# Hash attention followed by a squared-ReLU layer: where the first pair prepares the second pair

## The chip, the cores and the metric

The kernel runs on one core of a Trainium2 chip. The metric is the device time of one execution in microseconds (us). TensorE (PE in the profile) multiplies matrices, VectorE (DVE) and ScalarE (ACT) work element by element, GpSimd (POOL) does a little set-up, and SyncE (SP) issues most of the DMAs. Each engine works through its own instructions in the order in which they were issued[...].

## What is computed

The reference, cut to what matters (4 batches, 8 heads, 768 positions, head width 64, 6 hash bits; 3072 tokens, model width 512, hidden width 2048):

```python
q_bits = (np.einsum('bhsd,dk->bhsk', q, proj) > 0)
k_bits = (np.einsum('bhsd,dk->bhsk', k, proj) > 0)
q_bucket = np.sum(q_bits * powers, axis=-1)        # the same for k_bucket
mask = q_bucket[:, :, :, None] == k_bucket[:, :, None, :]
scores = scale * np.matmul(q, k.transpose(0, 1, 3, 2))
scores = np.where(mask, scores, -1000000000.0)
attn = softmax(scores)
attn_out = np.matmul(attn, v)
x = attn_out.transpose(0, 2, 1, 3).reshape(B * S, H * D)
h = x @ w_in
out = np.maximum(h, 0.0) ** 2 @ w_out
```

A query sees only the keys that have the same six sign bits as itself.

## The kernel before

The kernel has two stages. The first, some 335 us long, is the attention; the second multiplies its result by the two weight matrices. The change touches only the very beginning of the first stage.

**Pairs and blocks.** Two heads are treated together as a pair; there are NP = 16 pairs, and the loop at L606 runs over them. In a pair the 768 keys fall into six blocks of 128. `score(pr, kt)` (L386) makes the scores of one key block against all 768 queries: into a PSUM tile of 512 columns and one of 256 (per head), each from a product of the bit rows (`bits`, bf16) and a product of the features (`feat`, the transposed q and k). ScalarE then takes the exponential of each of the two tiles (L413) into a buffer `e`. `attend(pr, kt)` (L432) multiplies a block of `e` with the values `v_nat`. `add_up(pr, kt)` (L419) adds the blocks up on VectorE for the softmax's denominators; its first call, with kt = 1, adds blocks 0 and 1 (L423), and later calls add one more block (L428).

**What the next pair needs.** `features(pr, w)` (L330) transposes the loaded q (w = 0) or k (w = 1) of a pair on VectorE, into tiles with two buffers. `hash_bits(pr, banks)` (L337) multiplies both with the projection, four products for q and four for k, into one PSUM tile named `hash`. `signs` (L351) turns the result into bit rows with eight ScalarE activations. `weigh` (L379) scales the key bits, in place, with one more. Inside the loop, `prepare()` (L610) is `hash_bits` and `signs` for the pair that follows. For pair 0 itself this work is done ahead of the loop, with `first_features` and `first_keys`.

**PSUM.** The tiles named `st`, `hash`, `tot` and `tp` are all taken in turn from one set of three (`turn`, L104). A new one therefore waits until the third one before it has been read, as a rule by ScalarE.

**The order.** The order is written out by hand (`tc.manual_schedule()`, L584): every engine gets its instructions as the Python calls come. In pair 0 it is: scores of block 0, the second half of the first key bits, scores of block 1, `add_up(0, 1)`, `features(1, 0)` and `features(1, 1)`, `part_weight(0)` (two VectorE steps of a weight conversion, L143 and L147), scores of blocks 2 and 3, `prepare()`, `place_power(0)` (its two ScalarE steps, L160 and L161), `attend` for blocks 0 and 1, `add_up` for blocks 2 and 3, `round_weight(0)` (three VectorE steps, L171, L176, L179), `part_weight(1)`, scores of blocks 4 and 5, `weigh(1)`, `place_power(1)`, `attend` for blocks 2 and 3, `add_up` for blocks 4 and 5. Pair 1 begins with `features(2, w)`, `round_weight(1)` and the scores of its blocks 0 and 1; then `finish(0)` does `prepare()` for pair 2, the sums of the denominators (`tot`, L457) and the last two `attend` of pair 0.

**Data.** The q and k of pair 1 are loaded by `load_pair(1)` (L287): eight DMAs on SP's queue, ahead of the loop.

Of the kernel before, what the change touches and what calls it, by code (L numbers as in the profile page):

```python
# [34 lines left out]
def kernel(  # L35
# [68 lines left out]
    def turn(name):  # L104

        return ps_s.tile([P, 2, 512], FP32, name=name, tag="turn")
# [16 lines left out]
    def load_weight(i):  # L123
        src, r, c = pieces[i]
        if src.dtype != U64:
            goals[i] = goal(i)
            nc.sync.dma_start(out=goals[i], in_=src[r:r + P, c:c + PIECE])
            return
        raw = p_w.tile([P, PIECE, 2], U32, name="raw", bufs=3)
        nc.sync.dma_start(  # L130
            out=raw.rearrange("p f w -> p (f w)"),
            in_=src.bitcast(U32)[r:r + P, 2 * c:2 * (c + PIECE)],
        )
        raws[i] = raw
# [28 lines left out]
    def round_weight(i):  # L163

        raw = raws.pop(i, None)
        if raw is None:
            return keep_weight(i)
        goals[i] = goal(i)
        low, high = raw[:, :, 0], raw[:, :, 1]
        power, top = parts.pop(i)  # L170
        nc.vector.scalar_tensor_tensor(  # L171
            out=power, in0=high, scalar=0x80000000, in1=power,
            op0=ALU.bitwise_and, op1=ALU.bitwise_or,
        )
        one = top.bitcast(FP32)
        nc.vector.scalar_tensor_tensor(  # L176
            out=one, in0=low, scalar=2.0**-32, in1=top, op0=ALU.mult, op1=ALU.add,
        )
        nc.vector.scalar_tensor_tensor(  # L179
            out=goals[i], in0=one, scalar=2.0**-20, in1=power.bitcast(FP32),  # L180
            op0=ALU.mult, op1=ALU.mult,
        )
        keep_weight(i)
# [95 lines left out]
    def load_pair(pr):  # L279


        b, j = divmod(pr, PB)
        for src, name in ((q, "q_nat"), (k, "k_nat")):
            t = p_qk.tile([P, S], FP32, name=name)
            for g in range(4):
                h, e = divmod(g, 2)
                nc.sync.dma_start(  # L287
                    out=t[g * 32:(g + 1) * 32].rearrange("i (c d) -> i c d", d=32),
                    in_=src[b, 2 * j + h].rearrange("(c i) (e d) -> e i c d", i=32, e=2)[e],
                )  # L290
            nat[pr, name] = t
# [38 lines left out]
    def features(pr, w):  # L330

        feat[pr, w] = p_f.tile([P, S], FP32, name=f"feat{w}")
        nc.vector.transpose(out=feat[pr, w], in_=nat[pr, ("q_nat", "k_nat")[w]])
# [3 lines left out]
    def hash_bits(pr, banks, ws=(0, 1), cs=(0, 1)):  # L337


        for w in ws:  # L340
            hashed[pr, w] = banks
            for c in cs:
                g = 2 * w + c
                for h in range(2):
                    rows = slice(h * D, (h + 1) * D)
                    nc.tensor.matmul(  # L346
                        out=banks[g * NR_B:(g + 1) * NR_B, h, 0:HS], lhsT=projs[rows],
                        rhs=feat[pr, w][rows, c * HS:(c + 1) * HS], start=True, stop=True,
                    )

    def signs(pr, w):  # L351
        bits[pr, w] = t = all_bits[pr % 2][w]
        for c in range(2):
            at = slice((2 * w + c) * NR_B, (2 * w + c + 1) * NR_B)
            for h in range(2):
                nc.scalar.activation(  # L356
                    out=t[h * D:h * D + NR_B, c * HS:(c + 1) * HS], in_=hashed[pr, w][at, h, 0:HS],
                    func=ACTF.Sign, scale=HUGE, bias=lifts[at],
                )
# [19 lines left out]
    def weigh(pr):  # L379

        t = bits[pr, 1]
        nc.scalar.activation(out=t, in_=t, func=ACTF.Copy, scale=gains)
# [3 lines left out]
    def score(pr, kt):  # L386

        e = ring[len(weights) % NRING]
        weights[pr, kt] = e
        key = slice(kt * P, (kt + 1) * P)  # L390
        sts = []

        def products(st, lo, hi, src, first):
            for h in range(2):
                rows = slice(h * D, (h + 1) * D)
                nc.tensor.matmul(  # L396
                    out=st[:, h, 0:hi - lo], lhsT=src[pr, 1][rows, key],
                    rhs=src[pr, 0][rows, lo:hi], start=first, stop=not first,
                )


        if (pr, kt) == (0, 0):
            for lo, hi in CUTS:
                sts.append(turn("st"))
                products(sts[-1], lo, hi, feat, True)
        for i, (lo, hi) in enumerate(CUTS):
            if len(sts) <= i:
                sts.append(turn("st"))
                products(sts[i], lo, hi, bits, True)
                products(sts[i], lo, hi, feat, False)  # L410
            else:
                products(sts[i], lo, hi, bits, False)
            nc.scalar.activation(  # L413
                out=e[:, :, lo:hi], in_=sts[i][:, :, 0:hi - lo], func=ACTF.Exp, scale=scale
            )
# [107 lines left out]
    def sums_in(c):  # L523

        j, h = divmod(c, 2)
        t, at = ins[j], slice(h * NS, (h + 1) * NS)
        nf = NFT // 2
        sums = [p_t.tile([P, nf, NS], FP32, name=f"s_in{n}", bufs=2) for n in range(4)]
        sums_a(
            t[:, 0:nf, 0, at], t[:, nf:NFT, 0, at], t[:, 0:nf, 1, at], t[:, nf:NFT, 1, at], *sums  # L530
        )
        for n in range(4):
            put_factor(3 + n, c * NS, sums[n])
# [9 lines left out]
    def load_x(i):  # L543

        x = p_c.tile([P, NFT, NCH], FP32, name="x")
        nc.gpsimd.dma_start(out=x, in_=x_all[:, :, i * NCH:(i + 1) * NCH])
        xs[i] = x, [p_c.tile([P, 2, NCH // 2], FP32, name=f"t_x{n}") for n in range(3)]
# [23 lines left out]
    def finish(pr, beside=None):  # L571

        tot = turn("tot")
        if beside:
            beside()
        sum_up(pr, tot)
        if pr == NP - 1:
            sum_x(0, 2)
            sum_x(0, 3)
        for kt in (SB - 2, SB - 1):  # L580
            attend(pr, kt)
        spread(pr)

    with tc.manual_schedule():  # L584
# [21 lines left out]
        for pr in range(NP):  # L606
            a, b = 2 * pr, 2 * pr + 1
            more = pr + 1 < NP

            def prepare():  # L610

                hash_bits(pr + 1, turn("hash"))
                for w in (1, 0):
                    signs(pr + 1, w)


            if pr + 2 < NP:
                load_pair(pr + 2)
            if pr == X_0:
                load_x(0)  # L620
            if not more:
                sums_in(3)
            if more and pr > 0:
                for w in range(2):
                    features(pr + 1, w)
            if pr > 0:
                round_weight(b - 2)
                load_weight(b)
            score(pr, 0)
            if pr == 0:  # L630
                first_keys(1, turn("hash"))
            score(pr, 1)
            if pr > 0:
                finish(pr - 1, prepare if more else None)
            add_up(pr, 1)
            if pr == 0:
                for w in range(2):
                    features(1, w)
            if pr > 0:
                normalize(pr - 1)  # L640


            if pr == X_0 + 1:
                for n in range(2):
                    load_unit(n)
            part_weight(a)
            score(pr, 2)
            score(pr, 3)
            if pr == 0:
                prepare()  # L650
            elif more:
                weigh(pr + 1)
            place_power(a)
            attend(pr, 0)
            attend(pr, 1)
            for kt in (2, 3):
                add_up(pr, kt)
            if more:
                load_values(pr + 1)


            round_weight(a)
            part_weight(b)
            if more:
                load_weight(a + 2)
            score(pr, 4)
            score(pr, 5)
            if pr == 0:
                weigh(1)
            place_power(b)  # L670
            attend(pr, 2)
            attend(pr, 3)
            add_up(pr, 4)

            if pr not in sums:
                add_up(pr, 5)
            if pr in sums:
                sums_in(sums[pr])
# [801 lines left out]
```

## Time and profile before

| | |
|---|---|
| time, median of 4 runs | 884.41 us (883.28 to 885.53) |
| the profiled execution | 883.89 us, of which the span of the profile is 882.1 us |
| granted TensorE clock, mean | 0.997 |
| 12 to 17 us: busy PE, DVE, ACT | 4.91, 3.48, 3.94 of 5.00 us |
| 17 to 22 us | 4.40, 4.90, 3.62 |
| 22 to 27 us | 3.42, 2.01, 4.88 |
| 27 to 32 us | 5.00, 4.90, 4.21 |
| 32 to 37 us | 5.00, 4.79, 4.75 |

Pair 0 fills about the first 30 us of the span and pair 1 the next 20. The five windows show how the load stands on the engines around the place of the change; the granted clock is 1.00 in all five. In the timelines that are shown in the prediction, a row gives the start of a run of like instructions (us from the start of the span), the time from the start of the first to the end of the last, the engine, the line, the operation, the tiles written and read, the number, and in brackets for how long the engine was idle before and who, by the profile, released it.

### The profile page before, as it was taken

The numbers are of one execution on the slowest core, as the hardware profiler recorded it, in microseconds if no ns is written. First come the engines' busy times: TensorE is split into PE (matmuls) and PEld (weight loads), VectorE is DVE, ScalarE is ACT, GpSimd is POOL, SyncE is SP. The second block draws the span as 40 slices with busy tenths as digits, with TensorE's granted clock in tenths as the row PEclk, the third lists the DMA queues.
The fourth block names the chain that finished last, engine by engine and source line by source line (L and its number), as shares of the span: only waits on it lengthen the run. The fifth ranks groups of instructions, "written<-read, shape, count | busy, mean of one in ns | idle before, by whom it ended". The sixth has DMA issues, their size and how long they took to land.

```text
span 882.1 us, 12164 instructions
## 1 busy us (share of the span) xinstructions
PE 867.6 (98%) x4364; PEld 520.2 (59%) x4364; DVE 755.9 (86%) x1096; ACT 391.7 (44%) x673; POOL 107.0 (12%) x172
## 2 busy tenths in 40 slices
PE   8999999999999999999999999999999999999996
PEld 4444444444444444444688875556888755568885
DVE  5899999999999998888779978888889788888875
ACT  5988888888888861222211123332111233321110
POOL 2000000000000000564222021111100211110002
PEclk9999999999999999999999999999999999999998
DMA  9678779899778545989897775436857744455565
GB/s 183 128 151 134 195 183 189 181 280 208 153 166 187 160 143 194 305 258 289 283 350 246 183 162 171 160 116 228 291 144 186 172 157 156 129 166 153 158 176 102
DMA packets 224131, 167.09 MB, mean 189 GB/s; under 512 B 164448, under 2 KB 181344, under 8 KB 224064
## 3 DMA queue, kind: packets, MB, share of 16 engines
q1 hardware_dynamic: 189152, 87.19, 41.2%
q0 software_dynamic: 12528, 41.30, 15.1%
q10 hardware_dynamic: 22384, 37.76, 14.3%
q8 instruction: 36, 0.59, 0.3%
q14 instruction: 31, 0.25, 0.1%
HBM read 124.52 MB, written 41.68 MB: 188 GB/s over the span
## 4 chain that ended last, share of the span: by engine, by line
PE 95%; DVE 2%; ACT 1%; issue 1%; DMA 0%; DVEq 0%
PE acc L708 40%; PE st L396 17%; PE acc L927 16%; PE xo L438 13%; PE acc L880 5%; PE tot L457 2%; PE hash L346 1%; DVE total L428 1%; ACT e L413 1%; ACT bits L356 1%; PE xo L326 0%; PE tp L309 0%; DMA w_in<-s_in 0%; DVE out_piece L179 0%; DVE power L171 0%
## 5 line engine op out<-in xcount | busy, mean ns | idle before, releaser
L413 ACT ACTIVATE e<-st 128x1024 f32<-128x1024 f32 x192 | 145.2, 810 | 46.9 <-PE st L396 42.7
L396 PE MATMUL st<-feat,feat 64*128 64x512 f32 (+1 forms) x768 | 150.4, 483 | 0.0
L438 PE MATMUL xo<-e,v_nat 128*64 128x512 f32 (+1 forms) x768 | 134.8, 492 | 0.0
L708 PE MATMUL acc<-b,leaf 128*128 128x256 f32 x600 | 133.4, 379 | 1.1 <-issue 1.1
L708 PEld LDWEIGHTS acc<-b,leaf 128*128 128x128 f32 x600 | 113.7, 190 | 17.9 <-issue 2.7
L428 DVE TENSOR_TENSOR total<-total,e 128x1536 f32<-128x1536 f32 x61 | 107.2, 1757 | 4.4
L438 PEld LDWEIGHTS xo<-e,v_nat 128*64 128x64 f32 x768 | 51.3, 136 | 82.4 <-issue 75.3
L927 PE MATMUL acc<-t_x,w_unit 128*128 128x512 f32 x192 | 90.2, 592 | 0.0
L396 PEld LDWEIGHTS st<-feat,feat 64*128 64x128 f32 x768 | 66.0, 188 | 33.7 <-issue 24.1
L708 PE MATMUL acc<-t,leaf 128*128 128x256 f32 x336 | 76.2, 380 | 0.0
L356 ACT ACTIVATE bits<-hash,lifts 32x384 bf16<-32x384 f32 x120 | 68.6, 572 | 3.2 <-issue 1.3
L708 PEld LDWEIGHTS acc<-t,leaf 128*128 128x128 f32 x336 | 63.7, 190 | 9.1 <-DVE t L519 0.5
L792 DVE SCALAR_TENSOR_TENSOR b<-h 128x512 f32<-128x512 f32 x96 | 65.7, 691 | 3.0
L396 PE MATMUL st<-bits,bits 64*128 64x256 bf16 (+1 forms) x384 | 63.1, 325 | 1.8 <-ACT e L413 1.4
L927 PE MATMUL acc<-x,w_unit 128*128 128x512 f32 x128 | 60.2, 592 | 0.0
L708 PE MATMUL acc<-x,w_unit 128*128 128x512 f32 x128 | 56.6, 594 | 0.0
L708 PE MATMUL acc<-b_t,leaf 128*128 128x256 f32 x240 | 53.8, 379 | 0.0
L927 PEld LDWEIGHTS acc<-t_x,w_unit 128*128 128x128 f32 x192 | 36.5, 190 | 28.9 <-issue 26.8
L715 ACT COPY two<-acc 128x256 f32<-128x256 f32 (+1 forms) x29 | 12.5, 431 | 87.7 <-PE acc L708 63.0
L715 ACT COPY one<-acc 128x256 f32<-128x256 f32 (+1 forms) x29 | 12.5, 431 | 86.2 <-PE acc L708 57.7
L708 PEld LDWEIGHTS acc<-b_t,leaf 128*128 128x128 f32 x240 | 45.5, 190 | 6.2
L396 PEld LDWEIGHTS <-bits 64*128 64x128 bf16 x384 | 23.4, 93 | 41.6 <-issue 37.9
(161 smaller groups left out, 1170.4 us busy)
## 6 DMA issues: line engine op xcount, KB each, us to landing
leaf<-w_out ACTq DMA_DIRECT2D x142, 256.0 KB, 3.1
w_unit<-w_in SPq DMA_DIRECT2D x16, 640.0 KB, 4.0
raw<-in_moe_w_in_dram SPq DMA_DIRECT2D x16, 512.0 KB, 5.5
raw<-in_moe_w_out_dram SPq DMA_DIRECT2D x16, 512.0 KB, 4.4
w_unit<-w_in SPq DMA_DIRECT2D x8, 896.0 KB, 8.1
w_out<-sums POOLq DMA_DIRECT2D x16, 448.0 KB, 6.8
sum<-w_in SPq DMA_DIRECT2D x16, 448.0 KB, 4.8
v_nat<-in_v_dram SPq DMA_DIRECT2D x16, 384.0 KB, 4.4
```

What stands on the lines that cost most here:

```text
L346: nc.tensor.matmul(out=banks[g * NR_B:(g + 1) * NR_B, h, 0:HS], lhsT=projs[rows], rhs=feat[pr, w][rows, c * HS:(c + 1) * HS], start=True, ...
L356: nc.scalar.activation(out=t[h * D:h * D + NR_B, c * HS:(c + 1) * HS], in_=hashed[pr, w][at, h, 0:HS], func=ACTF.Sign, scale=HUGE, bias=li ...
L396: nc.tensor.matmul(out=st[:, h, 0:hi - lo], lhsT=src[pr, 1][rows, key], rhs=src[pr, 0][rows, lo:hi], start=first, stop=not first,)
L413: nc.scalar.activation(out=e[:, :, lo:hi], in_=sts[i][:, :, 0:hi - lo], func=ACTF.Exp, scale=scale)
L428: nc.vector.tensor_tensor(out=totals[pr], in0=totals[pr], in1=weights[pr, kt][:, :, 0:S], op=ALU.add)
L438: nc.tensor.matmul(out=xo[h * D:(h + 1) * D, lo:hi], lhsT=nat[pr, "v_nat"][:, h, kt * D:(kt + 1) * D], rhs=weights[pr, kt][:, h, lo:hi], s ...
L457: nc.tensor.matmul(out=tot[g * 32:(g + 1) * 32, 0:HS], lhsT=ones, rhs=src[:, h, c * HS:(c + 1) * HS], start=src is srcs[0], stop=src is sr ...
L708: nc.tensor.matmul(out=acc[to], lhsT=a(i), rhs=b(i), start=first and i == 0, stop=last and i == n - 1, skip_group_check=True,)
L715: nc.scalar.copy(out=t, in_=acc[of])
L792: nc.vector.scalar_tensor_tensor(out=out, in0=h, scalar=0.0, in1=h, op0=ALU.max, op1=ALU.mult)
L880: nc.tensor.matmul(out=out, lhsT=w[:, a], rhs=b, start=start, stop=stop, skip_group_check=True)
L927: nc.tensor.matmul(out=acc[to], lhsT=w[:, PLACE[a], f], rhs=bt[b](f), start=first and f == 0, stop=last and f == NFT // 2 - 1, skip_group_ ...
```

## The change

Two steps of pair 0 are moved; nothing is added or taken out. The two `features(1, w)` now stand ahead of `add_up(0, 1)` on VectorE. The `prepare()` for pair 1, which followed the scores of the fourth block (kt = 3), now stands ahead of them. For the other pairs the order is the same: the second hunk only rewrites the condition for `weigh`.

```diff
@@ -630,12 +630,12 @@
             if pr == 0:
                 first_keys(1, turn("hash"))
             score(pr, 1)
+            if pr == 0:
+                for w in range(2):
+                    features(1, w)
             if pr > 0:
                 finish(pr - 1, prepare if more else None)
             add_up(pr, 1)
-            if pr == 0:
-                for w in range(2):
-                    features(1, w)
             if pr > 0:
                 normalize(pr - 1)
 
@@ -645,10 +645,10 @@
                     load_unit(n)
             part_weight(a)
             score(pr, 2)
-            score(pr, 3)
             if pr == 0:
                 prepare()
-            elif more:
+            score(pr, 3)
+            if more and pr > 0:
                 weigh(pr + 1)
             place_power(a)
             attend(pr, 0)
```

In the two programs' instruction lists this gives: on TensorE the 8 hash products move ahead of the 8 score products (and their weight loads) of the fourth block; on ScalarE the 8 sign activations move ahead of the fourth block's two exponentials; on VectorE the two transposes move ahead of the first sum. GpSimd's and SP's lists are the same in both.

## The prediction

> **What bounds the kernel.** I read the page's busy shares and its chain first, then the timelines of TensorE, ScalarE and VectorE over the first 60 us.
>
> ```profile
> span 882.1 us, 12164 instructions
> PE 867.6 (98%) x4364; PEld 520.2 (59%) x4364; DVE 755.9 (86%) x1096; ACT 391.7 (44%) x673; POOL 107.0 (12%) x172
> PE 95%; DVE 2%; ACT 1%; issue 1%; DMA 0%; DVEq 0%
> ```
>
> TensorE is busy for 98% of the span, and the chain that ended last is 95% TensorE. So only TensorE's idle time, 14.5 us in all, can be won. Pair 0 holds part of it:
>
> ```profile
> 16.40 0.29 PE L396 MATMUL st<-bits,bits 64*128 64x256 bf16 x2
> 16.51 0.61 PE L396 MATMUL st<-feat,feat 64*128 64x256 f32 x4
> 17.72 1.62 PE L346 MATMUL hash<-feat,projs 64*32 64x384 f32 x16 [0.60 <-ACT e L413]
> 19.27 2.81 PE L438 MATMUL xo<-e,v_nat 128*64 128x512 f32 x16
> 22.01 0.39 PE L396 MATMUL st<-bits,bits 64*128 64x512 bf16 x2
> ...
> 24.17 0.39 PE L396 MATMUL st<-bits,bits 64*128 64x512 bf16 x2 [0.37 <-ACT bits L356]
> ...
> 26.63 0.29 PE L396 MATMUL st<-bits,bits 64*128 64x256 bf16 x2 [1.21 <-ACT e L413]
> ...
> 33.36 1.11 PE L346 MATMUL hash<-feat,projs 64*32 64x384 f32 x16
> 34.40 0.85 PE L457 MATMUL tot<-total,ones 128*32 128x384 f32 x8
> ```
>
> There are three waits: 0.60 us before the hash products (and a stretched 1.62 us for them), 0.37 before the sixth block's first tile, 1.21 before its second. The two other engines tell why:
>
> ```profile
> 13.38 4.75 ACT L413 ACTIVATE e<-st 128x1024 f32<-128x1024 f32 x6 [0.85 <-PE st L396]
> 19.45 4.66 ACT L356 ACTIVATE bits<-hash,lifts 32x384 bf16<-32x384 f32 x8 [1.32 <-issue]
> 24.14 0.72 ACT L160 ACTIVATE small<-power,excess 128x512 uint8<-128x512 uint32 x1
> 24.90 0.63 ACT L161 ACTIVATE power<-small 128x512 uint32<-128x512 uint8 x1
> 25.55 2.92 ACT L413 ACTIVATE e<-st 128x1024 f32<-128x1024 f32 x4
> ```
>
> ```profile
> 14.93 1.76 DVE L423 SCALAR_TENSOR_TENSOR total<-e,e 128x1536 f32<-128x1536 f32 x1 [1.47 <-ACT e L413]
> 16.60 0.97 DVE L333 STREAM_TRANSPOSE feat<-q_nat 128x768 f32<-128x768 f32 x1
> 17.50 0.94 DVE L333 STREAM_TRANSPOSE feat<-k_nat 128x768 f32<-128x768 f32 x1
> ```
>
> VectorE stood idle for 1.47 us, did the first sum, and only then the transposes, which end at 17.57 and 18.43. TensorE, through with the fourth block, could have begun the hash at about 16.95 (a block takes 15.33 to 13.71, 1.62 us, and this one began at 15.33). It began the q half at 17.72 and the k half only at 18.49, 0.05 after the k transpose. The profile names an exponential as the releaser of the first wait, but that tile's buffer was last read by the third block's second exponential, which ended at 16.51; it was the q transpose. The signs followed 0.96 after the k half began: ScalarE, which has work without a pause from 19.45, lost 1.32 us. The 1.21 us wait at 26.63 hangs on it: the sixth block's second tile needs the PSUM tile whose exponential started at 25.55, behind signs and power.
>
> **The change, part by part.** All durations come from this execution.
>
> *Transposes first (VectorE).* VectorE is free at 13.45. The last k DMA of pair 1 was issued at 8.33 and took 3.99 us to land, 12.3; the q ones are earlier. So the transposes run 13.46 to 15.29 (1.83 us, as before from 16.60 to 18.43). The first sum needs the second block's exponentials, done at 14.89; it goes from 14.92 to 15.22. Only VectorE waits for it. Then come part_weight(0) (0.72), whose data landed at 15.2, and the third block's sum, 17.5 to 19.3.
>
> *Hash between third and fourth block (TensorE).* The third block ends at 15.33; k is ready at 15.29 plus 0.05. The hash starts at 15.34 and takes 0.80 (pair 2 shows it unhindered: 53.50 to 54.30). Its buffer, the second block's, is free at 14.89. The fourth block goes from 16.14 to 17.76; its tiles come free at 16.02 and 16.51. The products with the values (2.74, from 19.27 to 22.01) end at 20.50.
>
> *Signs before the fourth block's exponentials (ScalarE).* They are ready at 15.34 + 0.96 = 16.30, while the third block's exponentials run until 16.51: no gap. Signs 16.53 to 21.19, the fourth block's exponentials to 22.8. From 13.38 to the fifth block's exponential ScalarE has the same work as before and no pause. So this exponential starts 1.32 earlier, at 24.23.
>
> *The price.* On TensorE the fifth block's first tile now takes the buffer of the hash, so it waits for the last sign: from 20.50 to about 21.25, a new wait of 0.75. It is covered, as the sixth block's second tile still waits for the fifth block's exponential: 26.63 less 1.32 = 25.31. Everything on TensorE from there stands 1.32 earlier; pair 1 begins at 28.70 instead of 30.02, its hash at 32.04 instead of 33.36. On VectorE the fourth block's sum stood ready at 20.85 and now waits for 22.8; behind it are queued round_weight(0), part_weight(1), two sums and the transposes of pair 2. It ends at 24.58. Then round_weight(0), whose power is there at 25.53 - 1.32 = 24.21, starts at 24.55 instead of 25.56. **VectorE wins only 1.0.**
>
> *What is late next.* Pair 1's hash waited for VectorE before: its k half could not start until the transpose was through at 33.56, and 34.40 - 33.36 is 1.04 against 0.80 unhindered, 0.24 lost. Now k is ready at 33.56 - 1.0 = 32.56 while TensorE arrives at 32.04. The loss grows to 32.56 + 0.05 - 32.04 = 0.57, so `tot` follows at 33.40 instead of 34.40. Sum: 1.32 - (0.57 - 0.24) = **1.0 us**. After it nothing holds the gain: in pair 2 VectorE waits 0.65 for TensorE, ScalarE up to 1.7, and all pairs and the second stage follow TensorE. SP's list is unchanged; the earlier transposes only free buffers that its loads reach at 22.3 anyway.
>
> **A rule that speaks against it.** The Trainium skill, "ScalarE: Activation LUTs", section "What ACT_TABLE_LOAD costs", says that each switch to another function set costs about 2.66 us (1283 ns and a drain). The change puts signs between exponentials: one more trip away from Exp and back, two switches. By the rule that is up to 5.3 us, and the sum becomes a loss of about 4. But the rows by line show ACT_TABLE_LOAD once in the whole span (1283 ns at 2.59 us), and between exponentials and signs of pair 1 only 0.08 us. The functions lie in one set here; I take zero.
>
> **Forecast and rivals.** Profiled execution 883.89, less 1.0: 882.9. The median stands 0.52 above it: 884.41 - 1.0 = **883.4 us**. What a measurement can tell from no change is 0.2%, 1.8 us.
>
> *A, as worked out, 0.55:* gain 0.9 to 1.35 (the upper end if VectorE doesn't hold pair 1's hash), 883.0 to 883.5.
>
> *B, more is won, 0.25:* besides the hash wait (18.49 - 16.95 = 1.54) the 0.37 goes too, 1.9 in all: 882.5, faster beyond 0.2%. All waits of pair 0 and pair 1's 0.24 give 3.4 at most, 881.0. For it: the signs are done almost 3 us earlier. Against: ScalarE's work up to the fifth block's exponential leaves no room for more than 1.32.
>
> *C, the hash is late, slower, 0.08:* TensorE works in order, so if k of pair 1 isn't there, the fourth block's scores, its exponentials and its sum all queue behind the hash, where before they passed ahead. Every us by which k is late after 15.3 costs one: the sum is nothing at a lateness of 1.0 (landing at about 15.4), and 0.2% slower at 2.8 (about 17.2), 886.2. For it: a k DMA took 3.5 to 5.6 us to land. Against: even 5.6 from 8.33 gives 13.9, before the 14.36 at which its transpose would begin.
>
> *D, nothing moves the end, 0.12:* VectorE in pair 1 takes the whole gain: if its fourth sum ends at 25.5 rather than 24.58, the hash of pair 1 is no earlier than before. 884.4.
>
> **The numbers.** Faster takes most of B and a little of A through scatter, 0.26; slower is C and a rest of D, 0.08; within 0.2% 0.66. The range, 882.0 to 884.9, holds A, D and B's 882.5, with the 1.1 us by which single runs of before lie off their median; it leaves out C and B's far end.
>
> **What would show it.** After: the transposes begin at 13.5 and the first sum near 15.2; hash products at 15.3 in about 0.8; no ScalarE pause ahead of the signs at 16.5; a new wait of 0.75 on TensorE at 20.5, one of about 1.3 ending at 25.3; pair 1's first scores at 28.7, its hash taking 1.3 to 1.4, `tot` at 33.4. Wrong if `tot` stands within 0.3 of 34.40 (D), or ahead of 32.9 (B), or if the transposes begin after 14 (C).

## The result and the profile after

The changed kernel takes 882.54 us, the median of 40 runs (881.82 to 883.62), against 883.88 us for the kernel before (60 runs, 883.12 to 885.53). The ratio is 0.9985, with a 95% interval of 0.9981 to 0.9990: between 0.9 and 1.7 us are won, a gain that is there but smaller than the 0.2% that was named as the bound.

The head of the page of the kernel after:

```profile
span 880.7 us, 12164 instructions
PE 866.6 (98%) x4364; PEld 519.7 (59%) x4364; DVE 755.7 (86%) x1096; ACT 391.7 (44%) x673; POOL 107.1 (12%) x172
```

The busy times are those of before to 1.0 us. From the second block's first scores to pair 2's `tot`, TensorE was busy for 40.03 of 42.21 us before and for 39.58 of 41.07 us after. So 0.69 us of idle time went; the other 0.45 had counted as busy, mostly because hash products that wait for their operand inside the group are counted so. In this execution pair 0 ran 0.34 us later than in the profile of before: the second block's first scores start at 12.43 and not at 12.09, behind a later load of pair 0's k. All times below are to be read against that. Three rows of TensorE's timeline of before that the prediction does not show (second block, pair 1's first scores, pair 2's `tot`):

```profile
12.09 0.39 PE L396 MATMUL st<-bits,bits 64*128 64x512 bf16 x2 [0.24 <-ACT e L413]
...
30.02 0.39 PE L396 MATMUL st<-bits,bits 64*128 64x512 bf16 x2
...
54.30 0.85 PE L457 MATMUL tot<-total,ones 128*32 128x384 f32 x8
```

TensorE's timeline of the kernel after, from there to pair 2's `tot`:

```profile
12.43 0.39 PE L396 MATMUL st<-bits,bits 64*128 64x512 bf16 x2 [0.22 <-ACT e L413]
...
15.78 0.88 PE L346 MATMUL hash<-feat,projs 64*32 64x384 f32 x16
...
21.60 0.39 PE L396 MATMUL st<-bits,bits 64*128 64x512 bf16 x2 [0.49 <-ACT bits L356]
...
25.46 0.29 PE L396 MATMUL st<-bits,bits 64*128 64x256 bf16 x2 [0.99 <-ACT e L413]
...
28.86 0.39 PE L396 MATMUL st<-bits,bits 64*128 64x512 bf16 x2
...
32.19 1.47 PE L346 MATMUL hash<-feat,projs 64*32 64x384 f32 x16
33.59 0.85 PE L457 MATMUL tot<-total,ones 128*32 128x384 f32 x8
...
53.50 0.85 PE L457 MATMUL tot<-total,ones 128*32 128x384 f32 x8
```

The hash runs without a wait in 0.88 us (before: a wait of 0.60 and then 1.62). The wait of 0.37 for the last sign, which stood before the sixth block, is replaced by one of 0.49 before the fifth, and pair 1's hash is stretched from 1.11 to 1.47 us. ScalarE's timeline shows where the gain is made:

```profile
13.72 3.13 ACT L413 ACTIVATE e<-st 128x1024 f32<-128x1024 f32 x4 [0.85 <-PE st L396]
16.88 4.67 ACT L356 ACTIVATE bits<-hash,lifts 32x384 bf16<-32x384 f32 x8
21.57 1.51 ACT L413 ACTIVATE e<-st 128x1024 f32<-128x1024 f32 x2
...
23.87 0.63 ACT L161 ACTIVATE power<-small 128x512 uint32<-128x512 uint8 x1
24.41 2.90 ACT L413 ACTIVATE e<-st 128x1024 f32<-128x1024 f32 x4
```

No bracket stands behind the signs any more: the 1.32 us of idling ahead of them are gone. VectorE's timeline shows the price, first before (the third and the fourth block's sums in one row, and pair 2's k transpose), then after:

```profile
19.00 3.61 DVE L428 TENSOR_TENSOR total<-total,e 128x1536 f32<-128x1536 f32 x2
...
32.63 0.93 DVE L333 STREAM_TRANSPOSE feat<-k_nat 128x768 f32<-128x768 f32 x1
```

```profile
13.72 0.97 DVE L333 STREAM_TRANSPOSE feat<-q_nat 128x768 f32<-128x768 f32 x1
14.62 0.94 DVE L333 STREAM_TRANSPOSE feat<-k_nat 128x768 f32<-128x768 f32 x1
...
23.12 1.76 DVE L428 TENSOR_TENSOR total<-total,e 128x1536 f32<-128x1536 f32 x1 [3.59 <-ACT e L413]
24.80 0.69 DVE L171 SCALAR_TENSOR_TENSOR power<-raw,power 128x512 uint32<-128x512 uint32 x1
...
31.83 0.94 DVE L333 STREAM_TRANSPOSE feat<-k_nat 128x768 f32<-128x768 f32 x1
```

The fourth block's sum waits 3.59 us for exponentials that stand behind the signs, and all that is queued behind it, down to the k transpose of pair 2 at 31.83, is late for TensorE, whose hash begins at 32.19 and gets its k at 32.77 only.

### The profile page after: what moved, and what is told of

It is laid out like the page before. It is cut to its first block, busy times and chain, and to the rows that moved or that the text cites. A ratio compares the mean times of both kernels' runs of the same rounds, so it can differ in the third digit from the quotient of the medians.

```text
span 880.7 us, 12164 instructions
## 1 busy us (share of the span) xinstructions
PE 866.6 (98%) x4364; PEld 519.7 (59%) x4364; DVE 755.7 (86%) x1096; ACT 391.7 (44%) x673; POOL 107.1 (12%) x172
## 4 chain that ended last, share of the span: by engine, by line
PE 94%; DVE 2%; ACT 1%; DMA 1%; issue 0%; ACTq 0%; DVEq 0%
PE acc L708 40%; PE st L396 17%; PE acc L927 16%; PE xo L438 13%; PE acc L880 5%; PE tot L457 2%; PE hash L346 2%; DVE total L428 1%; DMA k_nat<-in_k_dram 1%; ACT e L413 1%; ACT bits L356 1%; DMA w_in<-s_in 0%; DVE out_piece L179 0%; DVE power L171 0%; ACT small L160 0%
```

## The experiments

The differences are of the size of a run's scatter, so two readings are kept beside each other: the median (11 runs of each experiment, 40 of the full change) against the kernel before on the same chip, and, in one profiled execution, two stretches of TensorE's timeline. Both begin with the second block's first scores (12.09 in before); one ends with pair 1's first scores (30.02), the other with pair 2's `tot` (54.30). They leave out the start and the second stage, which differ from one execution to the next by some tenths of a us and more. Two programs were profiled in two executions each (the full change and e8); each gave its stretches again to 0.01 us.

| kernel | median, us | of before | ratio (95%) | to pair 1 | to pair 2's tot |
|---|---|---|---|---|---|
| before | 883.88 | | | 17.92 | 42.21 |
| full change | 882.54 | 883.88 | 0.9985 (0.9981 to 0.9990) | 16.42 | 41.07 |
| e1 transposes only | 882.35 | 883.83 | 0.9981 (0.9972 to 0.9990) | 16.64 | 40.91 |
| e2 hash only | 885.42 | 883.83 | 1.0017 (1.0008 to 1.0026) | 19.98 | 44.62 |
| e3 full, pair 2 early | 882.21 | 883.83 | 0.9979 (0.9970 to 0.9988) | 16.41 | 40.83 |
| e4 transposes, pair 2 early | 882.66 | 883.83 | 0.9984 (0.9975 to 0.9993) | 16.62 | 41.04 |
| e5 full, late loads | 884.77 | 883.79 | 1.0010 (1.0001 to 1.0019) | 18.38 | 43.03 |
| e6 before, late loads | 883.44 | 883.79 | 0.9996 (0.9987 to 1.0005) | 17.93 | 42.18 |
| e7 transposes, part early | 882.23 | 883.79 | 0.9981 (0.9972 to 0.9990) | 16.62 | 40.68 |
| e8 full, part between | 881.72 | 883.79 | 0.9978 (0.9969 to 0.9987) | 16.42 | 40.47 |
| e9 full change again | 882.59 | 883.65 | 0.9991 (0.9982 to 1.0000) | 16.42 | 41.07 |
| e10 as e8, again | 881.67 | 883.65 | 0.9977 (0.9968 to 0.9986) | 16.42 | 40.47 |

**Which half of the change does it?** First each half alone. e1 moves the transposes only:

```diff
             score(pr, 1)
+            if pr == 0:
+                for w in range(2):
+                    features(1, w)
...
             add_up(pr, 1)
-            if pr == 0:
-                for w in range(2):
-                    features(1, w)
```

> Only the two transposes of pair 1 are moved ahead of the first sum; the hash products stay behind the fourth block's scores. My theory (what is won is ScalarE's pause of 1.32 us ahead of the signs): the transposes end at about 15.3, so the hash runs at once behind the fourth block, near 17.0, and its result is there about when the fourth block's exponentials end at 18.1. The pause is gone as in the full change, and the fourth block's sum on VectorE doesn't wait for the signs, so pair 1's hash loses 0.24 us as before and not 0.56: 1.3 us faster than before, 0.15 to 0.3 us faster than the full change; on TensorE no wait of 0.5 before the fifth block's first tile. Rival (the place of the hash between the third and fourth block brings the gain): about as before, at most 0.5 us faster.

TensorE's timeline of e1, and the signs in ScalarE's:

```profile
17.14 0.88 PE L346 MATMUL hash<-feat,projs 64*32 64x384 f32 x16
...
22.97 0.39 PE L396 MATMUL st<-bits,bits 64*128 64x512 bf16 x2 [0.49 <-ACT bits L356]
...
32.16 1.09 PE L346 MATMUL hash<-feat,projs 64*32 64x384 f32 x16
```

```profile
18.24 4.67 ACT L356 ACTIVATE bits<-hash,lifts 32x384 bf16<-32x384 f32 x8
```

ScalarE's pause ahead of the signs is gone here too. The stretch to pair 2's `tot` is 1.30 us shorter than before, 0.16 shorter than with the full change, and pair 1's hash takes 1.09, about the 1.11 of before. The rival falls: the hash's new place is not what brings the gain. As expected, there is no wait before the fifth block's first tile; the wait for the last sign (0.49) stands at the sixth block's first tile (22.97), where before had 0.37. The e2 kernel moves the other half:

```diff
             score(pr, 2)
-            score(pr, 3)
             if pr == 0:
                 prepare()
-            elif more:
+            score(pr, 3)
+            if more and pr > 0:
                 weigh(pr + 1)
```

> Only the hash products and signs are moved between the third and the fourth block's scores; the transposes stay behind the first sum and end at 18.43. My theory: the hash can't start its k half before 18.49, the fourth block's scores queue behind it on TensorE and its exponentials behind the signs (24.1), so the fifth block's exponential starts at about 27.0 in place of 25.55: 1.5 to 2.0 us slower than before. Rival (the hash's new place brings the gain): faster by 0.5 us or more.

```profile
17.69 2.28 PE L346 MATMUL hash<-feat,projs 64*32 64x384 f32 x16 [2.21 <-DVE feat L333]
```

```profile
20.08 4.66 ACT L356 ACTIVATE bits<-hash,lifts 32x384 bf16<-32x384 f32 x8 [3.59 <-issue]
```

In these rows of TensorE's and ScalarE's timelines of e2 the hash waits 2.21 us for the q transpose. Its k half begins at 18.46, 0.05 after the k transpose, but the signs follow only 1.62 later, where before they followed after 0.96. Beside the missing 0.66 stands a lower clock: in windows of 1 us the granted clock is 1.00 up to 18 us, 0.75 from 18 to 19, 0.50 from 19 to 21, 0.54 from 21 to 22, and 1.00 again after. In no other trace of the twelve is it under 1.00 in the first 56 us. With the fourth block's scores queued behind the hash, pair 1 starts some 2.05 late, and pair 2's `tot` follows 2.42 late. Less the 0.66, an estimate, that would be about 1.8, within the expected 1.5 to 2.0; the median shows 1.6 (0.7 to 2.3). In how many of the eleven runs the clock fell here is not known. Placed without its operands, the hash does harm in any case.

**Does VectorE take back a part?** Both halves together reach pair 1 at 16.42, earlier than the transposes alone (16.64), and yet come to pair 2's `tot` later. If VectorE's late fourth sum is the cause, then an earlier k transpose for pair 2 must give the difference back. e3 and e4 move pair 2's two transposes ahead of the sixth block's sum, on top of the full change and of e1:

```diff
-            if more and pr > 0:
+            if more and pr > 1:
                 for w in range(2):
                     features(pr + 1, w)
...
             add_up(pr, 4)
+            if pr == 0:
+                for w in range(2):
+                    features(2, w)
             if pr not in sums:
                 add_up(pr, 5)
```

> The full change, and the transposes for pair 2 moved from the head of pair 1 to between the fifth and the sixth block's sums of pair 0 on VectorE. My theory (VectorE's late sum takes 0.3 us or more back at pair 1's hash): k of pair 2 is ready 1.8 us earlier, pair 1's hash takes 0.8 to 0.9 in place of 1.47, and the kernel is 0.5 to 0.6 us faster than the full change, 1.7 us faster than before. Rival (the longer hash of pair 1 is paid back in pair 2 anyway): as the full change within 0.15 us, 1.2 us faster than before.

> The transposes of pair 1 ahead of the first sum, the hash products where they were before, and the transposes for pair 2 between the fifth and sixth block's sums. My theory: ScalarE's 1.32 and the 0.24 of pair 1's hash are both won, 1.5 to 1.6 us faster than before, about as the run with the full change and early transposes for pair 2. Rival (only the hash's place counts): as before within 0.5 us.

Neither gave a clear answer. Pair 1's hash took 0.88 us in both, as meant, and `tot` of pair 1 stood 1.75 (e3) and 1.53 us (e4) earlier than before. But some 0.36 us of that were gone again by pair 2's `tot`. TensorE's timeline of e4 shows a wait that no kernel before had:

```profile
36.90 1.02 PE L396 MATMUL st<-feat,feat 64*128 64x512 f32 x4
38.10 0.29 PE L396 MATMUL st<-bits,bits 64*128 64x256 bf16 x2 [0.19 <-ACT bits L356]
```

The third block's second tile of pair 1 waits for the last sign, as if it had got the buffer of the hash. In the built programs it has: in e3 and e4 it is given the hash's PSUM buffer, in all the others that of `tot`, which VectorE has read by 34.75 in e4, over 3 us before the last sign. The buffers are handed out when the kernel is built; how the build chooses was not looked into. So the sentence "the third one before it" holds as a rule only, and a move on VectorE had changed the waits of TensorE. e7 and e8 therefore win the time on VectorE in another way, with the buffers as they were: in pair 0 the two steps of `part_weight(1)` (0.67 us from the first one's start to the next instruction's, 26.73 to 27.40 in the full change) go into VectorE's idle time. For e8, on top of the full change:

```diff
             for kt in (2, 3):
                 add_up(pr, kt)
+                if (pr, kt) == (0, 2):
+                    part_weight(b)
...
             round_weight(a)
-            part_weight(b)
+            if pr > 0:
+                part_weight(b)
```

> The full change, and in pair 0 part_weight(1) moved between the third and the fourth block's sums, into VectorE's 3.6 us of waiting. k of pair 2 is ready 0.75 us earlier; the PSUM tiles get the same buffers as in the full change. My theory (VectorE's late sum takes 0.6 us back at pair 1's hash): that hash takes 0.88 in place of 1.47, the signs behind it start 0.4 earlier, and the kernel is 0.5 to 0.6 us faster than the full change, 1.7 us faster than before, faster than any kernel so far. Rival (ScalarE is the bound of pair 1 anyway and takes the 0.6 back): as the full change within 0.2 us.

In e7, on top of e1, `part_weight(1)` stands directly ahead of `round_weight(0)`.

> Only the transposes of pair 1 moved (the hash products where they were), and in pair 0 part_weight(1) moved ahead of round_weight(0), into VectorE's 3.2 us of waiting for ScalarE's power. k of pair 2 is ready 0.75 us earlier; the PSUM tiles get the same buffers as before. My theory: pair 1's hash takes 0.88 in place of 1.09 and the 0.2 us stay: 1.5 us faster than before. Rival (ScalarE's signs of pair 1 are the bound and take the 0.2 back): as the transposes alone, 1.3 us faster than before.

VectorE's and TensorE's timelines of e8:

```profile
19.32 0.42 DVE L143 TENSOR_SCALAR power<-raw 128x512 uint32<-128x512 uint32 x1
...
22.98 1.76 DVE L428 TENSOR_TENSOR total<-total,e 128x1536 f32<-128x1536 f32 x1 [2.90 <-ACT e L413]
...
31.02 0.94 DVE L333 STREAM_TRANSPOSE feat<-k_nat 128x768 f32<-128x768 f32 x1
```

```profile
32.05 0.88 PE L346 MATMUL hash<-feat,projs 64*32 64x384 f32 x16
32.86 0.85 PE L457 MATMUL tot<-total,ones 128*32 128x384 f32 x8
```

The wait of the fourth sum is shorter by the work put into it (2.90, not 3.59), the k transpose ends at 31.96, before the hash begins, and the hash takes 0.88 in place of 1.47. The stretch to pair 2's `tot` is 40.47, 0.60 less than with the full change; to pair 1 it is the same 16.42. In e7 it is 0.23 less than in e1. Nothing is lost later: from the second block's first scores to the first products of the second stage it is 322.60 us before, 321.46 with the full change, 321.30 in e1 and 320.86 in e8, the same differences as at pair 2's `tot`. So it is shown that pair 1's hash waited for VectorE's queue, that this cost the full change 0.60 us and e1 0.23, and that ScalarE doesn't take it back.

**What if the data are late?** The rival on the slow side was a late k. e5 and e6 issue pair 1's loads behind the values and two weight pieces:

```diff
-        load_pair(1)
         load_values(0)
         for i in range(2):
             load_weight(i)
+        load_pair(1)
```

> The full change, with the loads of pair 1's q and k issued behind those of the values and of the first two weight pieces. k lands at about 16.5 in place of 12.3, so its transpose ends near 17.5 and not at 15.3. My theory: the full change hands every us of lateness on, since the fourth block's scores, exponentials and sum queue behind the hash: about 2.2 us slower than the full change, so 0.8 to 1.2 us slower than before. Rival (the work behind the hash fills the gap, or later waits take the lateness up): at most 0.5 us slower than the full change, still faster than before.

> The kernel before with the same late loads. There k is transposed from 17.5 only, when it has landed at 16.5: my theory says the time of before within 0.3 us, either way. Rival (late loads cost something whatever the order, at the start of pair 0 or on SP's queue): slower than before by the same 2 us as in the full change.

VectorE's timeline of e5, and the hash in TensorE's:

```profile
16.55 0.98 DVE L333 STREAM_TRANSPOSE feat<-k_nat 128x768 f32<-128x768 f32 x1 [1.67 <-DMA k_nat<-in_k_dram]
```

```profile
17.58 0.85 PE L346 MATMUL hash<-feat,projs 64*32 64x384 f32 x8 [1.25 <-DVE feat L333]
```

k's transpose begins at 16.55, when its load has landed, and ends at 17.53. Against the full change, where it ended at 15.56 with the loop 0.30 us later, that is 2.27 us late; pair 1 and pair 2's `tot` are both 1.96 later. The full change loses its gain and is slower than before by 1.0 us (0.1 to 1.7). The old order with the same loads is unharmed, 42.18 in place of 42.21. The mechanism of the rival is real and costs nearly one for one (1.96 for 2.27); only, with the loads as they were, no trace shows a transpose of pair 1 that waits for its data.

**The best version, once more.** The full change and e8 were run side by side on one chip.

> The full change once more, beside the next run on the same chip. My theory: 1.1 to 1.4 us faster than before; from the second block's first scores to pair 2's tot 41.07 us as in its first trace, within 0.1.

> The full change with part_weight(1) of pair 0 between the third and fourth block's sums, once more, beside the full change on the same chip. My theory: the 0.6 us seen in the trace from the second block's scores to pair 2's tot (40.47 in place of 41.07) are there again, and the median lies 0.3 to 0.9 us below the full change's. Rival: the two medians lie within 0.2 us.

Both stretches came out again to 0.01 us. The medians are 882.59 and 881.67, 0.92 us apart; e8's kernel is 0.23% faster than before (0.14% to 0.32%), more than the full change in both of its comparisons. The intervals of the two kernels overlap a little, but side by side ten of e8's eleven runs lie below the fastest of the full change (882.25). The traces account for 0.60 of the 0.92; the rest is not explained.

## Why the prediction came out as it did

*The misread wait.* That the transpose, and not an exponential, released the hash is confirmed: with the transposes moved and nothing else (e1), the wait is gone.

*ScalarE's pause, put at 1.32 us.* Right in kind, somewhat small: up to pair 1 TensorE won 17.92 - 16.42 = 1.50. The rest lies in the joints between ScalarE's instructions, which I had taken as equal. Before, `power` ended at 25.53 and the exponential began at 25.55; after, it ended at 24.50 and the exponential had begun at 24.41. One pause of 0.1 us in which an exponential waited for the fourth block's scores went as well.

*The covered wait of 0.75 before the fifth block.* It came, smaller, with 0.49, ended by the last sign at 21.60 (my 21.25 with the late start), and it was covered as worked out: what held TensorE was the wait that ended at 25.46, by the fifth block's exponential.

*VectorE wins only 1.0, and the hash of pair 1 grows from 1.04 to 1.37.* This was the step that set the sum apart from the plain 1.32. The fourth sum ran from 23.12, where I had 22.8 plus the 0.34; the hash to `tot` took 33.59 - 32.19 = 1.40; 1.50 - 1.14 = 0.36 were given back, where I had 0.33. e8 shows it by taking it away.

*The sum.* 1.14 us in the stretch against 1.0. It is what VectorE won: pair 2's k transpose, which sets `tot`, begins 1.14 earlier in the stretch (32.63 - 12.09 = 20.54, and 31.83 - 12.43 = 19.40). Half of the 0.14 over the forecast lies in one joint of VectorE: `round_weight(0)` began 1.68 after the fourth sum did, at 24.80, where I had taken 1.75. In the medians the gain is 1.34 in the first comparison and 1.06 in the second. The forecast of 883.4 stood on a median of 884.41 from four runs; the 60 runs of before give 883.88, so half a us of the distance to the measured 882.54 is the base and not the change. That the median now lies at B's 882.5 is an accident of this base: the gain is the one named under A.

*Only idle time can be won.* This sentence of the prediction was too narrow: 0.45 of the 1.14 us had counted as busy. The working itself did price the stretched hash.

*The rivals.* B needed 1.9 us and fell at the place named against it: ScalarE's work leaves about 1.5. D fell, as `tot` moved. C did not occur, but e5 shows its price. ScalarE's table loads, which the rule would have charged with up to 5.3 us, did not show: the trace after has again a single ACT_TABLE_LOAD, the signs begin 0.03 us after the exponentials end (13.72 + 3.13 to 16.88), and the exponentials 0.02 after the signs.

What I did not see was that the second half of the change isn't needed for the gain, which the prediction's own numbers would have told. With the transposes alone the hash could have started at 16.95, its result been there at 17.9, and the fourth block's exponentials ended at 18.13: no pause either, and no late sum. I worked out only the change as it stood.

## What to carry to other kernels

If a pause of one engine is traced to a late operand, price the earlier operand alone before moving its consumer too: here it won 1.30 us by itself; the consumer's move added 0.2 up to pair 1, on ScalarE, and cost 0.4 behind it, on VectorE. If a step is moved ahead on engines that work in order, write down who is queued behind what it displaces (here a sum, a conversion and the next pair's transposes), and fill the new wait with work that is ready. And where buffers are handed out by the build, look after every move at who gets which: a step moved on one engine can give another a new wait.

## What the runs showed beyond that

In the two programs that were profiled twice, the stretch of TensorE's timeline to pair 2's `tot` is the same to 0.01 us in both executions, while whole executions of one kernel scatter over 1.8 us and more (881.82 to 883.62); so a part of it lies in the start, where the k of pair 0 landed earlier or later (with the loads as they were, the second block's scores began between 11.98 and 12.48), and in the second stage: from the second block's scores to TensorE's end e8's kernel took 861.2 us in one execution and 860.1 in the other, with the first 320.86 us, to the end of the attention, alike to 0.01 us. For gains of a tenth of a per cent, a stretch of one trace told more than eleven timed runs, provided that the granted clock is looked at beside it, as e2 shows.
